# A decode step with two attention layers: the last head group's P.V split between rows and columns, and a new order around the softmax

## The chip, the cores and the metric

The kernel runs on one core of a Trainium2 chip. Its time is the device time of one execution in microseconds (us), and the median of three runs is quoted. A profile is one separate execution: its *span* runs from the first to the last instruction that the profiler recorded, and the execution's own time is a little longer. The engines are TensorE (PE, with its weight loads shown as PEld), VectorE (DVE), ScalarE (ACT), GpSimd (POOL) and SyncE (SP). SP issues every large load here, in one in-order queue (SPq in the profile). Sixteen DMA engines move the bytes.

## The reference

One token (batch 1, sequence 1, width 640) passes attention, an MLP block, the same attention again and the same block again. Weights and caches are the same both times.

```
W = 4096                                  # last W positions of the caches
q = (x @ wq).reshape(32 heads, 192)
k, v = k_cache[:, :, Sk-W:, :], v_cache[:, :, Sk-W:, :]
p = softmax(q . k * 192**-0.5)            # per head, over W
x = x + (p . v).reshape(6144) @ wo        # A, on layernorm(x)
x = x + B(layernorm(x))                   # B: x1 + gelu(layernorm(x1) @ w3) @ w4
x = x + A(...); x = x + B(...)            # second layer, same again
```

With a sequence of one position the shifts inside B move only padding zeros into place, so its first half adds nothing. Per head, K and V are 4096 x 192 bf16 each, 1536 KB. There are 32 heads and two layers.

## The kernel before

**Tiling.** The heads form eight groups of four (`G = 4`). A slot is an SBUF tile of 128 partitions x 6144 elements, which holds one head's K or V, 32 positions to a partition. There are fifteen slots; five hold `wq` for good. SP loads K and V into slots in a planned order (`plan`, L604): for each group the K of the next group and the V of this one alternate, with the 960 KB of `wo` in the middle, and the MLP weights `w34` (L125 to L138) last. `half` is a tile of half a slot; it holds the softmax's work areas (E, ET, O_lo, O_sb and one of two buffers of P) and, at the end of a layer, the last part of `w4`: L135 loads over E, L136 over the rest.

**One head's keys.** `trans` (L297) turns K on DVE in 32 x 32 blocks, in two halves of 128 x 1536 (L305). It writes into a spare slot, and K's slot is the spare of the next head. `kmm` (L326) multiplies with twelve matmuls (L331) into the scores S_ps, and its end frees the turned slot.

**The softmax of one group.** `soft_a`: maximum (L347), mask (L349), transpose on PE (L351), negated maximum (L353). `soft_b`: bias back to all partitions (L359, copied at L361), exponential into E with its sum (L363). `soft_c`: E is transposed on DVE (L369), sixteen small matmuls arrange P (L378), ACT copies it to SBUF as PT (L384), and the sum's reciprocal is taken (L386 to L390).

**P.V has two forms.** In rows (`pv_rows`, L426), 16 matmuls per head have eight columns of P as weights and stream V (L435, 128 x 384 each). The results of all heads of a group add up in one PSUM tile; `norm_rows` prepares the factors, and `evac_rows` (L465) evicts with ACT (L467, O_lo) and DVE (L468, O_sb), turns the result by f32 matmuls (L471 to L477) and casts it (L480). In columns (`pv_cols`, L396), V is the weights: 64 matmuls of one column each (L409, L415, L420), and a pair of heads is evicted by three short DVE instructions (`evac_cols`, L444). `outproj` (L483) multiplies a pair of heads with `wo`, 15 matmuls (L487).

**The order.** The schedule is written by hand: each engine takes its instructions in program order. While group g has its P.V in rows, the next group's keys are turned and multiplied, one head against one. Then come `soft_a` of the next group, both halves of the first K of the group after it, P.V of g's fourth head, `soft_b`, `evac_rows(g)`, both `outproj(g)`, and `soft_c`. The last group of a layer has all four heads in columns, with an eviction and an `outproj` after every second. The addition of L568 ends the attention; `mixer` (L570) does the MLP, with 60 matmuls on `w3` (L581) and 60 on `w4` (L598).

**Between the layers.** The second layer takes the groups backwards, so group 7 comes last and then first: its V and its turned K stay in eight slots. Two slots hold `w34`. No key can be loaded for the next layer until `mixer` has read `w3` and `w4` out of those two (L584, L601), and the next slots come free as `kmm` of group 7 ends, head by head. At this start (`warm`) the order is: `kmm` of four heads, `soft_a`, the query projection of the next group (L277 to L288), `soft_b`, both halves of the next group's first K, `soft_c`.

Of the kernel before, what the change touches and what calls it, by code (L numbers as in the profile page):

```python
# [8 lines left out]
BF16 = mybir.dt.bfloat16  # L9
F32 = mybir.dt.float32  # L10
U32 = mybir.dt.uint32
# [5 lines left out]
P = 128  # L17
G = 4
# [7 lines left out]
def kernel(  # L26
# [14 lines left out]
    nc = tc.nc  # L41
# [9 lines left out]
    J = W // P  # L51
    S4 = 4
    NJQ = J // S4
    NFB = Dh // 64
# [5 lines left out]
    HJ = J // 2  # L60
    HALF = FREE // 2
# [232 lines left out]
    T_t = {}  # L294
    spent = [None]

    def trans(h):  # L297
        Kn = resident.pop(("K", h))
        T = spent.pop()
        if T is None or T not in free:  # L300
            T = free.pop()
        else:
            free.remove(T)
        for hf in range(2):
            nc.vector.transpose(  # L305
                T[:, hf * HALF:(hf + 1) * HALF].bitcast(U32).rearrange(
                    "p (f j k) -> p j f k", f=NFB, j=HJ, k=32),
                Kn[:, hf * HALF:(hf + 1) * HALF].bitcast(U32).rearrange(
                    "p (j f k) -> p j f k", f=NFB, j=HJ, k=32))
        T_t[h] = T  # L310
        free.append(Kn)
        spent.append(Kn)
# [4 lines left out]
    def kmm(g, i):  # L317
        h = g * G + i
        if i == 0:
            S_t[g] = S_two[nS[0] % 2]  # L320
            nS[0] += 1
        S_ps = S_t[g]
        T = T_t[h]
        x, par = i // 2, i % 2
        n = 0
        for f in range(NFB):  # L326
            for t in range(2):
                for hf in range(2):
                    Tv = T[:, hf * HALF:(hf + 1) * HALF].rearrange("p (f c t) -> p f c t", f=NFB, t=2)
                    r = 32 * (2 * par + hf)  # L330
                    nc.tensor.matmul(  # L331
                        S_ps[r:r + 8, :], lhsT=Q_t[g][:, x, par * NCOL + 2 * f + t, :], rhs=Tv[:, f, :, t],
                        start=(x == 0 and n == 0), stop=(n == NCOL - 1), tile_position=(0, r),
                        skip_group_check=True)
                n += 1
        if h not in keep_T:
            free.append(T_t.pop(h))
# [26 lines left out]
            out=E, in_=S_ps[:], func=ACTF.Exp, bias=nb_sb[:, 0:1], scale=scale, accum_out=lpart[:, 0:1])  # L364
        sx[g].update(lpart=lpart)

    def soft_c(g):
        d = sx[g]
        nc.vector.transpose(  # L369
            ET.rearrange("p (j r) -> p j r", r=32), E.rearrange("p (j k) -> p j k", k=32))  # L370
        ETv = ET.rearrange("p (j u m) -> p j u m", u=8, m=4)
        Pv = Pp_ps[:].rearrange("p (x par hf j c) -> p x par hf j c", x=2, par=2, hf=2, c=8)
        for tl in range(4):
            par, hf = tl // 2, tl % 2
            for m in range(4):
                one = Pv[32 * m:32 * (m + 1), 0, par, hf, :, 2 * par:2 * par + 2]
                two = bass.AP(one.tensor, one.offset, [one.ap[0], [2 * G * J + 4, 2], *one.ap[1:]])
                nc.tensor.matmul(  # L378
                    two, lhsT=identb[:, 32 * tl:32 * (tl + 1)],
                    rhs=ETv[:, :, 0:2, m].rearrange("p (j e) x -> p x j e", e=2), start=True, stop=True,  # L380
                    tile_position=(0, 32 * m), skip_group_check=True)
        PT = PT_two[nP[0] % 2]
        nP[0] += 1
        nc.scalar.copy(PT, Pp_ps[:])  # L384
        lsel = sm.tile([P, G], F32, name="lsel")
        nc.vector.tensor_scalar(out=lsel[:], in0=hs[:], scalar1=d["lpart"][:, 0:1], scalar2=None, op0=ALU.mult)  # L386
        l_ps = psm.tile([P, G], F32, tag="psm", name="l_ps")
        nc.tensor.matmul(l_ps[:], lhsT=ones[:], rhs=lsel[:], start=True, stop=True)  # L388
        rl = sm.tile([P, G], F32, name="rl")
        nc.vector.reciprocal(rl[:], l_ps[:])  # L390
        d.update(rl=rl, PT=PT.rearrange("p (g j c) -> p g j c", g=G, c=8))

    O_t = {}
    nO = [0]

    def pv_cols(g, i, keep):  # L396
        h = g * G + i
        if i == 0:
            O_t[g] = O_two[nO[0] % 2]
            nO[0] += 1  # L400
        O_ps = O_t[g][:, 0:8].rearrange("p (a b) -> p a b", a=2)
        V = resident[("V", h)]
        PT = sx[g]["PT"]
        pr, odd = i // 2, i % 2
        oa = TB if odd else 0
        col = lambda j: PT[:, i, j // 2, 2 * i + j % 2:2 * i + j % 2 + 1]
        ca, cc = (3, 2) if odd else (0, 1)
        for j in range(J):
            nc.tensor.matmul(  # L409
                O_ps[:, pr, ca:ca + 1], lhsT=V[:, j * Dh + oa:j * Dh + oa + P], rhs=col(j),  # L410
                start=(j == 0), stop=(j == J - 1))
        r0 = TB if odd else 0
        oc = 0 if odd else P
        je = 0 if odd else J - 1
        nc.tensor.matmul(  # L415
            O_ps[r0:r0 + TB, pr, cc:cc + 1], lhsT=V[:, je * Dh + oc:je * Dh + oc + TB], rhs=col(je),
            start=True, stop=False, tile_position=(0, r0), skip_group_check=True)
        js = [j for j in range(J) if j != je]
        for j in js:
            nc.tensor.matmul(  # L420
                O_ps[:, pr, cc:cc + 1], lhsT=V[:, j * Dh + oc - r0:j * Dh + oc - r0 + P], rhs=col(j),
                start=False, stop=(j == js[-1]), skip_group_check=True)
        if not keep:
            free.append(resident.pop(("V", h)))

    def pv_rows(g, i, keep):  # L426
        h = g * G + i
        if i == 0:
            O_t[g] = O_two[nO[0] % 2]
            nO[0] += 1  # L430
        V = resident[("V", h)]
        PT = sx[g]["PT"]
        for jj in range(J // 2):
            r = 32 * (jj % 4)
            nc.tensor.matmul(  # L435
                O_t[g][r:r + 8, :], lhsT=PT[:, i, jj, :],
                rhs=V[:, jj * 2 * Dh:(jj + 1) * 2 * Dh], start=(i == 0 and jj < 4),
                stop=(i == G - 1 and jj >= J // 2 - 4), tile_position=(0, r), skip_group_check=True)
        if not keep:
            free.append(resident.pop(("V", h)))  # L440

    osb_t = {}

    def evac_cols(g, pr):  # L444
        if pr == 0:
            osb_t[g] = sm.tile([P, 2, 3], BF16, name="osb")
        osb, rl = osb_t[g], sx[g]["rl"]
        O_ps = O_t[g][:, 0:8].rearrange("p (a b) -> p a b", a=2)
        nc.vector.tensor_tensor(  # L449
            out=osb[:, pr, 0:3:2], in0=O_ps[:, pr, 0:4:3], in1=rl[:, 2 * pr:2 * pr + 2], op=ALU.mult)  # L450
        nc.vector.tensor_tensor(
            out=osb[0:TB, pr, 1:2], in0=O_ps[0:TB, pr, 1:2], in1=rl[0:TB, 2 * pr:2 * pr + 1], op=ALU.mult)
        nc.vector.tensor_tensor(
            out=osb[TB:P, pr, 1:2], in0=O_ps[TB:P, pr, 2:3], in1=rl[TB:P, 2 * pr + 1:2 * pr + 2], op=ALU.mult)
# [39 lines left out]
    def attention(order, xT_cur, xT_new, keep, loads):  # L494
# [13 lines left out]
        where = {what: n for n, what in enumerate(loads)}  # L508
        ahead = lambda *what: need(where.get(what, -1) + 1)

        def keys(h):
            if h not in T_t:
                ahead("K", h)
                trans(h)

        tot_ps, rstd = ln_stats(xT_cur)
        xn_bf = sm.tile([P, ND], BF16, name="xn_bf")
# [10 lines left out]
        if warm:  # L528
            need(G + 1)
        soft_a(g0)  # L530
        if warm:
            qproj(g1, xn_bf)
        soft_b(g0)
        if warm:
            keys(g1 * G)
        soft_c(g0)
        for n, g in enumerate(order):
            nxt = order[n + 1] if n + 1 < len(order) else None
            for i in range(G):
                if nxt is not None:  # L540
                    keys(nxt * G + i)
                    kmm(nxt, i)
                    if i == G - 1:
                        soft_a(nxt)
                        if n + 2 < len(order):
                            keys(order[n + 2] * G)
                ahead("V", g * G + i)
                if i == 1 and n + 2 < len(order):
                    qproj(order[n + 2], xn_bf)
                if nxt is not None:  # L550
                    if i == 0:
                        norm_rows(g)
                    pv_rows(g, i, ("V", g * G + i) in keep)
                    continue
                pv_cols(g, i, ("V", g * G + i) in keep)
                if i % 2 == 1:
                    evac_cols(g, i // 2)
                    ahead("wo", g)
                    outproj(g, i // 2, y_ps, n == 0 and i == 1, i == G - 1)
            ahead("wo", g)  # L560
            if nxt is not None:
                soft_b(nxt)
                evac_rows(g)
                outproj(g, 0, y_ps, n == 0, False)
                outproj(g, 1, y_ps, False, False)
                soft_c(nxt)
        need(len(loads))
        nc.vector.tensor_tensor(out=xT_new[:], in0=xT_cur[:], in1=y_ps[:], op=ALU.add)  # L568

# [99 lines left out]
```

## Time and profile before

| | us |
|---|---|
| median of 3 runs | 547.46 (547.16 to 548.74) |
| the profiled execution, own time | 548.08 |
| its span | 546.3 |
| PE busy / DVE busy / ACT busy | 321.1 / 272.9 / 35.3 |
| one half of a K transpose (L305), x120 | 1.751 each, 205.3 in all |
| bytes moved | 218.80 MB, mean 401 GB/s over the span |

Times inside the profile count from the span's start. "Idle before" a group is time in which its engine stood still just ahead of it, with what ended the wait. The granted TensorE clock is a share of full speed. A matmul's recorded duration holds pipeline time, so for a run of matmuls the distance from start to start tells more.

### The profile page before, as it was taken

What the parts mean: (1) busy time and instruction counts of PE and PEld (TensorE: products, weight loads), DVE (VectorE), ACT (ScalarE), POOL (GpSimd) and SP (SyncE); (2) the same over time, 40 slices, a digit from 0 to 9 for tenths busy, and PEclk for the clock granted to TensorE, in tenths of its full rate; (3) what the DMA queues carried; (4) which work ended last, traced back from release to release, by engine and by line L of the source; (5) the groups of instructions that cost most, each with busy time, mean ns of one, the idle gap of its engine ahead of it and who ended that gap; (6) DMA issues with size and microseconds to landing.
All of it is one profiled execution on the core that took longest, in us unless ns stands there. A gap on an engine that the chain in (4) does not pass through costs nothing.

```text
span 546.3 us, 8648 instructions
## 1 busy us (share of the span) xinstructions
PE 321.1 (59%) x3851; PEld 158.5 (29%) x3851; DVE 272.9 (50%) x394; ACT 35.3 (6%) x111; POOL 2.1 (0%) x11
## 2 busy tenths in 40 slices
PE   1164765675754667365575576766654667365575
PEld 0011232241322214131174233332322224131164
DVE  4176555555636545454312476775636545454312
ACT  1001010000100001010001001010100001010001
POOL 1000000000000000000000000000000000000000
PEclk9998757665577756557655677778677756557655
DMA  8999999999999999999996889999999999999992
GB/s 350 429 425 412 423 426 414 426 413 423 415 424 425 413 426 411 428 413 421 416 400 250 326 353 428 425 414 422 412 426 426 411 427 412 425 414 425 413 398 79
DMA packets 33833, 218.80 MB, mean 401 GB/s; under 512 B 2692, under 2 KB 16516, under 8 KB 17796
## 3 DMA queue, kind: packets, MB, share of 16 engines
q1 hardware_dynamic: 33786, 218.25, 97.0%
q8 instruction: 30, 0.49, 0.4%
q14 instruction: 7, 0.06, 0.0%
q10 hardware_dynamic: 10, 0.00, 0.0%
HBM read 218.24 MB, written 0.00 MB: 399 GB/s over the span
## 4 chain that ended last, share of the span: by engine, by line
DMA 53%; PE 21%; DVE 19%; issue 4%; SPq 1%; ACT 1%; DVEq 0%
DMA slot<-in_A_k_cache_dram 53%; DVE slot L305 14%; PE S_ps L331 9%; PE O_ps L435 2%; DVE pm L347 2%; PE O_ps L420 1%; PE O_ps L409 1%; SPq L108 1%; PE y_ps L487 1%; PE nb_ps L359 1%; PE qT_ps L277 1%; PE pmT_ps L351 1%; PE hT_ps L581 1%; PE y2T_ps L598 1%; DVE pmh L349 1%
## 5 line engine op out<-in xcount | busy, mean ns | idle before, releaser
L305 DVE STREAM_TRANSPOSE slot<-slot 128x1536 uint32<-128x1536 uint32 x120 | 205.3, 1751 | 78.9 <-DMA slot<-in_A_k_cache_dram 78.9
L331 PE MATMUL S_ps<-slot,Q 128*8 128x512 bf16 x768 | 170.4, 550 | 118.5 <-DVE slot L305 116.7
L331 PEld LDWEIGHTS <-Q 128*8 128x8 bf16 x768 | 42.8, 102 | 215.8 <-issue 203.3
L435 PE MATMUL O_ps<-slot,half 128*8 128x384 bf16 x512 | 61.4, 444 | 0.0
L435 PE MATMUL O_ps<-slot,PT 128*8 128x384 bf16 x384 | 42.0, 424 | 0.0
L347 DVE TENSOR_REDUCE pm<-S_ps 128x1 f32<-128x512 f32 x16 | 11.1, 691 | 42.4 <-PE S_ps L331 42.4
L361 ACT COPY nb_sb<-nb_ps 128x1 f32<-128x1 f32 x16 | 2.5, 159 | 399.4 <-PE nb_ps L359 399.4
L471 PE MATMUL OT_ps<-ho,half 128*128 128x2 f32 x28 | 8.0, 356 | 34.0 <-DVE half L468 34.0
L281 DVE TENSOR_TENSOR Xq<-qT_ps,maskq 128x24 bf16<-128x24 f32 x16 | 2.9, 182 | 48.6 <-PE qT_ps L277 48.6
L435 PEld LDWEIGHTS <-half 128*8 128x8 bf16 x512 | 19.4, 98 | 20.9 <-issue 17.6
L277 PE MATMUL qT_ps<-xn_bf,slot 128*128 128x1 bf16 x480 | 15.2, 164 | 14.0 <-DMA slot<-in_A_wq_dram 11.6
L277 PEld LDWEIGHTS <-slot 128*128 128x128 bf16 x480 | 13.8, 98 | 20.8 <-DMA slot<-in_A_wq_dram 13.3
L487 PE MATMUL y_ps<-osb,wo_g 128*128 128x1 bf16 x480 | 15.7, 165 | 4.7 <-DVE osb L480 3.7
L435 PEld LDWEIGHTS <-PT 128*8 128x8 bf16 x384 | 13.5, 97 | 15.4 <-issue 12.6
L487 PEld LDWEIGHTS <-wo_g 128*128 128x128 bf16 x480 | 15.9, 104 | 4.8 <-issue 4.5
L471 PEld LDWEIGHTS OT_ps<-ho,half 128*128 128x128 f32 x28 | 6.8, 303 | 35.2 <-DVE half L468 35.2
L351 PE MATMUL pmT_ps<-ident,pmh 128*4 128x128 f32 x16 | 5.2, 327 | 18.3 <-DVE pmh L349 18.3
L449 DVE TENSOR_TENSOR osb<-O_ps,rl 128x2 bf16<-128x2 f32 x4 | 0.6, 162 | 23.5 <-PE O_ps L420 23.5
L480 DVE CAST osb<-OT_ps 128x6 bf16<-128x6 f32 x14 | 2.3, 164 | 19.8 <-PE OT_ps L477 19.8
L390 DVE RECIPROCAL rl<-l_ps 128x4 f32<-128x4 f32 x16 | 2.9, 182 | 18.2 <-PE l_ps L388 18.2
L369 DVE STREAM_TRANSPOSE half<-half 128x512 bf16<-128x512 bf16 x16 | 11.2, 700 | 1.5 <-ACT half L363 1.5
L409 PE MATMUL O_ps<-PT,slot 128*128 128x1 bf16 x256 | 8.4, 165 | 5.5 <-issue 5.2
(116 smaller groups left out, 212.7 us busy)
## 6 DMA issues: line engine op xcount, KB each, us to landing
slot<-in_A_k_cache_dram SPq DMA_DIRECT2D x60, 1536.0 KB, 23.8
slot<-in_A_v_cache_dram SPq DMA_DIRECT2D x60, 1536.0 KB, 23.8
wo_g<-in_A_wo_dram SPq DMA_DIRECT2D x14, 960.0 KB, 28.5
slot<-in_A_wq_dram SPq DMA_DIRECT2D x5, 1536.0 KB, 13.0
slot<-in_B_w_dram SPq DMA_DIRECT2D x2, 1536.0 KB, 23.5
slot<-in_B_w_dram SPq DMA_DIRECT2D x2, 1120.0 KB, 19.5
half<-in_B_w_dram SPq DMA_DIRECT2D x2, 640.0 KB, 8.6
slot<-in_B_w_dram SPq DMA_DIRECT2D x2, 384.0 KB, 18.0
```

What stands on the lines that cost most here:

```text
L108: nc.sync.dma_start(t[:], (Kw if kind == "K" else Vw)(h))
L277: nc.tensor.matmul(qT_ps[:, tl:tl + 1], lhsT=wq_t[kc][:, t * P:(t + 1) * P], rhs=xn_bf[:, kc:kc + 1], start=(kc == 0), stop=(kc == ND - 1))
L305: nc.vector.transpose(T[:, hf * HALF:(hf + 1) * HALF].bitcast(U32).rearrange("p (f j k) -> p j f k", f=NFB, j=HJ, k=32), Kn[:, hf * HALF:( ...
L331: nc.tensor.matmul(S_ps[r:r + 8, :], lhsT=Q_t[g][:, x, par * NCOL + 2 * f + t, :], rhs=Tv[:, f, :, t], start=(x == 0 and n == 0), stop=(n ...
L347: nc.vector.tensor_reduce(out=pm[:], in_=S_t[g][:], op=ALU.max, axis=AX.X)
L349: nc.vector.tensor_scalar(out=pmh[:], in0=off[:], scalar1=pm[:, 0:1], scalar2=None, op0=ALU.add)
L351: nc.tensor.transpose(pmT_ps[0:G, :], pmh[:, 0:G], ident[:, :])
L369: nc.vector.transpose(ET.rearrange("p (j r) -> p j r", r=32), E.rearrange("p (j k) -> p j k", k=32))
L409: nc.tensor.matmul(O_ps[:, pr, ca:ca + 1], lhsT=V[:, j * Dh + oa:j * Dh + oa + P], rhs=col(j), start=(j == 0), stop=(j == J - 1))
L435: nc.tensor.matmul(O_t[g][r:r + 8, :], lhsT=PT[:, i, jj, :], rhs=V[:, jj * 2 * Dh:(jj + 1) * 2 * Dh], start=(i == 0 and jj < 4), stop=(i = ...
L471: nc.tensor.matmul(OT_ps[:, :, 0], lhsT=O_sb[:, 0:P], rhs=ho[:, 0:4:2], start=True, stop=True, skip_group_check=True)
L487: nc.tensor.matmul(y_ps[:, n:n + 1], lhsT=wo_t[g][:, 3 * pr + t, n * P:(n + 1) * P], rhs=osb[:, pr, t:t + 1], start=(first and t == 0 and ...
```

## The change

`trans` becomes `trans_begin` and `trans_end`, one half each, so that other DVE work can stand between the halves. `soft_c` takes the head whose second half it issues after the matmul of the sum. In the loop over groups the softmax of the next group is issued before the eviction and output product of this one: `soft_b` right after `soft_a`, ahead of the fourth P.V, and `soft_c` ahead of `evac_rows`. In the warm start, `soft_b` comes ahead of the query projection.

```
+            if i == G - 1:
+                soft_a(nxt)
+                soft_b(nxt)
+                if ahead_h is not None:
+                    keys(ahead_h, whole=False)      # first half only
             ...
+                pv_rows(g, i, kept(g, i))
             ahead("wo", g)
-            if nxt is not None:
-                soft_b(nxt)
-                evac_rows(g)
-                outproj(g, 0, ...); outproj(g, 1, ...)
-                soft_c(nxt)
+            soft_c(nxt, ahead_h)                    # second half inside
+            evac_rows(g)
+            if ahead_h is not None:
+                outproj(g, 0, ...); outproj(g, 1, ...)
```

The last group of a layer (`gz`; `g` is the one before it, whose output product is still to come) is taken out of the loop:

```
+        for i in range(2):
+            ahead("V", gz * G + i)
+            pv_rows(gz, i, kept(gz, i), n_heads=2)
+        outproj(g, 0, ...); outproj(g, 1, ...)
+        ahead("wo", gz)
+        norm_rows(gz)
+        ahead("V", gz * G + 2)
+        pv_cols(gz, 2, kept(gz, 2))
+        evac_rows(gz)
+        outproj(gz, 0, ...)
+        ahead("V", gz * G + 3)
+        pv_cols(gz, 3, kept(gz, 3))
+        evac_cols(gz, 1)
+        outproj(gz, 1, ...)
```

Rows and columns use the two O_ps buffers, one each. `evac_cols` gets an `osb` tile of its own. The warm start:

```
         soft_a(g0)
-        if warm:
-            qproj(g1, xn_bf)
         soft_b(g0)
         if warm:
-            keys(g1 * G)
-        soft_c(g0)
+            keys(g1 * G, whole=False)
+            qproj(g1, xn_bf)
+        soft_c(g0, g1 * G)
```

The loads and their slots stand in the same order on SP's queue. Only what two of them wait for differs: L136 overwrites O_lo and O_sb, whose last use is now the eviction of `gz` instead of `g`.

More of the change, by code (lines that the diff above doesn't have):

```diff
@@ L295, with trans_half, trans_begin @@
     spent = [None]
-    def trans(h):
+    half_t = {}
+    def trans_half(Kn, T, hf):
+        nc.vector.transpose(
+            T[:, hf * HALF:(hf + 1) * HALF].bitcast(U32).rearrange(
+                "p (f j k) -> p j f k", f=NFB, j=HJ, k=32),
+            Kn[:, hf * HALF:(hf + 1) * HALF].bitcast(U32).rearrange(
+                "p (j f k) -> p j f k", f=NFB, j=HJ, k=32))
+    def trans_begin(h):
         Kn = resident.pop(("K", h))
@@ L303, in trans, with trans_end @@
             free.remove(T)
[L304 to L309, printed above, removed]
+        trans_half(Kn, T, 0)
+        half_t[h] = (Kn, T)
+    def trans_end(h):
+        Kn, T = half_t.pop(h)
+        trans_half(Kn, T, 1)
         T_t[h] = T
@@ L365, in soft_b, with soft_c @@
         sx[g].update(lpart=lpart)
-    def soft_c(g):
+    def soft_c(g, h_next=None):
         d = sx[g]
@@ L388, in soft_c @@
         nc.tensor.matmul(l_ps[:], lhsT=ones[:], rhs=lsel[:], start=True, stop=True)
+        if h_next in half_t:
+            trans_end(h_next)
         rl = sm.tile([P, G], F32, name="rl")
@@ L394 @@
     nO = [0]
+    Oc_t = {}
     def pv_cols(g, i, keep):
         h = g * G + i
-        if i == 0:
-            O_t[g] = O_two[nO[0] % 2]
+        if g not in Oc_t:
+            Oc_t[g] = O_two[nO[0] % 2]
             nO[0] += 1
-        O_ps = O_t[g][:, 0:8].rearrange("p (a b) -> p a b", a=2)
+        O_ps = Oc_t[g][:, 0:8].rearrange("p (a b) -> p a b", a=2)
         V = resident[("V", h)]
@@ L424, in pv_cols, with pv_rows @@
             free.append(resident.pop(("V", h)))
-    def pv_rows(g, i, keep):
+    def pv_rows(g, i, keep, n_heads=G):
         h = g * G + i
@@ L437, in pv_rows @@
                 rhs=V[:, jj * 2 * Dh:(jj + 1) * 2 * Dh], start=(i == 0 and jj < 4),
-                stop=(i == G - 1 and jj >= J // 2 - 4), tile_position=(0, r), skip_group_check=True)
+                stop=(i == n_heads - 1 and jj >= J // 2 - 4), tile_position=(0, r), skip_group_check=True)
         if not keep:
@@ L444, in evac_cols @@
     def evac_cols(g, pr):
[L445 to L448, printed above, removed]
+        osb, rl = sm.tile([P, 2, 3], BF16, name="osb"), sx[g]["rl"]
+        osb_t[g] = osb
+        O_ps = Oc_t[g][:, 0:8].rearrange("p (a b) -> p a b", a=2)
         nc.vector.tensor_tensor(
@@ L509, in attention, with keys @@
         ahead = lambda *what: need(where.get(what, -1) + 1)
-        def keys(h):
-            if h not in T_t:
+        def keys(h, whole=True):
+            if h not in T_t and h not in half_t:
                 ahead("K", h)
-                trans(h)
+                trans_begin(h)
+            if whole and h in half_t:
+                trans_end(h)
         tot_ps, rstd = ln_stats(xT_cur)
@@ L530, in attention @@
         soft_a(g0)
-        if warm:
-            qproj(g1, xn_bf)
         soft_b(g0)
         if warm:
-            keys(g1 * G)
-        soft_c(g0)
-        for n, g in enumerate(order):
-            nxt = order[n + 1] if n + 1 < len(order) else None
-            for i in range(G):
-                if nxt is not None:
[L541 to L546, printed above, removed]
+            keys(g1 * G, whole=False)
@@ new lines, in attention @@
+            qproj(g1, xn_bf)
+        soft_c(g0, g1 * G)
+        kept = lambda g, i: ("V", g * G + i) in keep
+        for n, g in enumerate(order[:-1]):
+            nxt = order[n + 1]
+            ahead_h = order[n + 2] * G if n + 2 < len(order) else None
+            for i in range(G):
+                keys(nxt * G + i)
+                kmm(nxt, i)
+                if i == G - 1:
[3 more added lines that the diff above has]
+                        keys(ahead_h, whole=False)
@@ L547, in attention @@
                 ahead("V", g * G + i)
-                if i == 1 and n + 2 < len(order):
+                if i == 1 and ahead_h is not None:
                     qproj(order[n + 2], xn_bf)
[L550 to L559, printed above, removed]
+                if i == 0:
+                    norm_rows(g)
@@ L560, in attention @@
+                pv_rows(g, i, kept(g, i))
             ahead("wo", g)
-            if nxt is not None:
-                soft_b(nxt)
-                evac_rows(g)
+            soft_c(nxt, ahead_h)
+            evac_rows(g)
+            if ahead_h is not None:
                 outproj(g, 0, y_ps, n == 0, False)
                 outproj(g, 1, y_ps, False, False)
-                soft_c(nxt)
+        gz = order[-1]
+        for i in range(2):
+            ahead("V", gz * G + i)
+            pv_rows(gz, i, kept(gz, i), n_heads=2)
@@ L567, in attention @@
+        outproj(g, 0, y_ps, False, False)
+        outproj(g, 1, y_ps, False, False)
+        ahead("wo", gz)
[3 more added lines that the diff above has]
+        evac_rows(gz)
+        outproj(gz, 0, y_ps, False, False)
+        ahead("V", gz * G + 3)
+        pv_cols(gz, 3, kept(gz, 3))
+        evac_cols(gz, 1)
+        outproj(gz, 1, y_ps, False, True)
+        Oc_t.clear()
         need(len(loads))
```

## The prediction

> **What bounds the kernel now.** I read first the page's 40 slices, one slice 13.66 us.
>
> ```profile
> DMA  8999999999999999999996889999999999999992
> GB/s 350 429 425 412 423 426 414 426 413 423 415 424 425 413 426 411 428 413 421 416 400 250 326 353 428 425 414 422 412 426 426 411 427 412 425 414 425 413 398 79
> ```
>
> Inside a layer the DMA engines are full. They are not in slices 21 to 23 (between the layers) and in the last one. Next, stretches of 2 us there; the last two columns are DMA share and GB/s.
>
> ```profile
> 290.00:292.00 2.00, 0.59 (x2) 0.53 (x3) 0.63 (x4) 0.95 (x6) 0.00 (x0) 0.50 0.45 151
> 292.00:294.00 2.00, 1.74 (x60) 1.65 (x59) 0.44 (x3) 0.12 (x1) 0.00 (x0) 0.50 0.03 12
> 294.00:296.00 2.00, 0.41 (x16) 0.43 (x16) 0.91 (x5) 0.28 (x2) 0.00 (x0) 0.50 0.57 123
> 302.00:304.00 2.00, 2.00 (x20) 0.74 (x20) 0.00 (x0) 0.00 (x0) 0.00 (x0) 0.50 0.42 178
> 304.00:306.00 2.00, 2.00 (x28) 0.62 (x20) 0.00 (x0) 0.00 (x0) 0.00 (x0) 0.50 0.45 74
> 318.00:320.00 2.00, 1.67 (x15) 0.35 (x7) 1.30 (x1) 0.00 (x0) 0.00 (x0) 0.52 0.56 129
> ```
>
> Summing 1 minus the share over 288 to 320 us gives 8.6 us of idle DMA, in three holes: until L581 and L598 have read `w3` and `w4`, until `kmm` of group 7 frees slots, and until 317.8, when the first V can be issued. After 320 the share is 1.0 to the end of loads. So before 320 and after the last K, compute sets the time; in between, bytes do. The chain of waits from the last K:
>
> ```profile
> 513.40 0.70 DVE pm L347
> 514.88 1.38 PE O_ps L435 x16
> 516.26 0.53 PE nb_ps L359 x2
> 517.78 0.32 ACT half L467
> 518.12 0.43 DVE half L468
> 518.60 0.59 PE OT_ps L471 x2
> 520.19 0.94 PE y_ps L487 x30
> 521.13 0.38 PE Pp_ps L378 x14
> 521.53 0.59 ACT PT L384
> 524.92 1.53 issue
> 530.91 1.74 issue
> 535.33 0.17 DVE x L568
> ```
>
> The path from the scores to PT holds the previous group's fourth P.V, its eviction and its output product. Then four heads in columns pass, with two "issue" holes. The same stretch between the layers starts at 267.69 and ends at 289.45 (21.76 us against 21.93 here), with holes of 1.16 and 1.95.
>
> **The holes.** Counted in the built program's list of PE instructions, weight loads included, they stand at rows 3102 and 3358, and in the tail at 6776 and 7032: 256 rows apart, each time. The page's queue q8 shows 30 instruction packets for 0.49 MB, about 16 KB each, which is 256 times 64 bytes. So I read them as blocks of instructions that arrive late: from one crossing to the next is 6.2 us (280.93 to 287.13, 526.45 to 532.64) where PE could use up a block in 4.
>
> The Trainium skill, "Runtime: NRT & Kernel Launch" (Instruction fetch mechanics), has the same blocks of 256 but calls a crossing "mostly hidden". By it the holes would be something else, and would stay: 3.1 and 3.3 us less gain, some 546.5 in all. The rows decide here, since the distances fit.
>
> **The change, step by step, in the tail (times of before).**
> 1. L359 no longer waits for 16 matmuls of P.V: L353 ends at 514.92 + 0.28 = 515.20, L359 can start at 515.30 instead of 516.26: **-0.96**.
> 2. From the end of the exponential (517.78) to the cast L384 (521.53) are 3.75 us. After: transpose to first L378 0.72 (313.44 to 314.16 in the warm start), to the cast 0.47 (314.16 to 314.63), 0.06 of hand-over: 1.25. **-2.50**. PT is there at 522.12 - 3.46 = 518.66.
> 3. What was moved comes now: L467 0.41, L468 0.43 and hand-overs 0.11: 519.61. Then the turn, 518.60 to 519.95 without its cast, 1.3: 520.9. Two heads in rows, 2 x 1.38 (above): 523.67. L487 x30, 0.94: 524.6.
> 4. V of the third head. The landings are issue plus landing time: `wo` 493.56 + 27.5 = 521.1, the fourth V 506.1 + 22.4 = 528.5, so the third in the middle, 524.8. A wait of 0.3: 524.9.
> 5. Columns of head 3: 0.99 + 0.14 + 0.92, less 0.1 of overlap, 1.95: 526.85. The turn of the two row heads up to its first L487 is 1.59 (518.60 to 520.19): 528.45, its 15 matmuls 0.5: 528.95. The eviction's ACT and DVE part hides under L487 and the columns; uncovered it costs 0.95.
> 6. Columns of head 4, 2.05, three evictions to first L487 0.24, L487 0.65 and hand-over 0.02: 531.9, against 535.33: **-3.4**.
>
> The two holes are gone in this sum: 188 PE rows fewer per layer (two heads of 126 rows become 32). The next crossings fall 256 rows before the old ones, in the third head's columns (525.25) and at the last L487 (530.9). These are 5.7 us apart where 6.2 were needed: bounds 0 to 1.95 (the longest hole) a place, I take 0.1 to 0.5 in the tail and 0 between the layers, where the crossing falls into the first L487, 6.8 us after the one before.
>
> Changes between tile shapes (rows, columns, f32 turn): three more a place. The nearest row is L415, which takes 0.14 where its neighbours take 0.03: 0 to 0.33, inside the rounding of steps 3 and 5. By "TensorEngine Tiling (Array Packing)" (Key Properties) a change of tiling mode drains the array; it gives no time, and its sum would be this upper bound.
>
> **The edge of the stream.** `mixer` moves up by 3.4 too. L581 would start at 534.6; the last part of `w3` lands at 515.39 + 18.0 = 533.4. The last 24 of L598 would start at 542.43 - 3.4 = 539.0; L136 lands at 529.79 + 8.8 = 538.6:
>
> ```profile
> half<-in_B_w_dram SPq DMA_DIRECT2D x1, 640.0 KB, 8.8
> ```
>
> L136 now waits for the turn of the last group, about 528.2, before its issue at 529.79: 1.6 us to spare. So the tail can give at most 542.43 - 538.6 = 3.8.
>
> **Between the layers** the same sum gives 286.1 for 289.45: -3.35. The third V (251.18 + 27.8 = 279.0) and the fourth (262.2 + 20.6 = 282.8) come at the edge again, L136 at 284.47 + 8.4 = 292.9 against 293.2. Then the warm start. Before, the query projection, two halves (310.08, 3.43), and L369 follow one another; `kmm` of group 6 starts at 315.02. After: maximum known at 308.91, half one until 310.65, Xq, Qrep and Q until 311.5, L369 0.70, L386 0.19, half two 312.4 to 314.1; the exponential (310.45) and the projection run beside it. `kmm` starts at 314.15: **-0.87**. The first V's issue, which ends the third hole, moves with it. So 3.35 + 0.87 = 4.2 of the 8.6 us of idle DMA go, and the whole stream after it comes 4.2 earlier. Its lower bound is 0 (a hole refilled elsewhere). An upper one: `kmm` of group 7, 5.44 us at clock 0.50, took half at a clock near 1, 2.7 more.
>
> **Inside a layer** I cost the new order at nothing. The half that waits for K, and with it E's transpose, L378 and P.V, queues behind it on DVE as the whole did before; on PE, P.V of the fourth head waits about 0.9 behind L359, so one V slot is free 0.9 later. Cover: a load takes 23.8 us from issue to landing where its own transfer takes 3.7 (1536 KB at some 425 GB/s), 20 us of queue. If that were gone, 14 turns of 0.9 cost 12.6.
>
> **Sum.** 546.3 - 3.4 + 0.2 (the tail's crossing) - 4.2 = 538.9 of span. The profiled run's own time was 548.08, 0.6 above the median; taken from the median, 547.46 - 7.4 = **540.1**.
>
> **Rivals.**
> - *The stream's edge binds* (0.10): the V of heads 3 and 4 and L136 land later than worked out, or L136 loses its 1.6 us. For it: four landings within 0.5 us of use. Against: the same stream in the same order. With 2 us lost at each place: 544.1.
> - *The gain between the layers is refilled* (0.10): holes stay, as slots and not compute end them. For it: the third hole ends with a slot. Against: that slot waits for `kmm`, which moves. Tail alone: 547.46 - 3.2 = 544.3.
> - *The stream starves inside the layers* (0.04), the slower side: half one stands ahead of E's transpose on DVE and waits for K (longest wait 5.4), so PT, P.V and slot returns come late in 13 groups. It decides from 0.6 us a group (13 x 0.6 = 7.8 eats the gain); at 1.5 a group: 547.46 - 7.4 + 19.5 = 559.6. Against: the 20 us of queue.
>
> **How the numbers follow.** My forecast has 0.76, with 538.0 (faster clock, no waits) to 542.5 (one long hole at one place, edges 0.5 late). The rivals at 544 lie just above, so the range stops at 543. A run of this kernel can't tell less than 0.3% (1.6 us) from no change; both milder rivals are beyond that. Faster 0.94, within 0.3% 0.02, slower 0.04.
>
> **What would show it.** L568 to L347 (21.8) falls to about 18.5 in both places; no "issue" hole above 0.6 in P.V; idle DMA between the layers about 4.4; the last K lands near 503; share 1.0 inside the layers. Wrong if holes reappear at other rows, if L598 waits for L136, or if DVE's waits for K grow while the share falls below 1.

## The result and the profile after

The changed kernel takes 540.11 us (median of four runs, 538.62 to 540.43) against 547.31 us (545.67 to 548.74) for the kernel before: a ratio of 0.9864, 95% interval 0.9831 to 0.9897. On another chip the ratio was 0.9864 again (0.9845 to 0.9884). The forecast was 540.1 us, with a range of 538.0 to 543.0. The profiled execution has a span of 537.6 us against 546.3.

The page's 40 slices of the changed kernel (13.44 us each):

```profile
DMA  8999999999999999999999899999999999999995
GB/s 345 430 424 411 423 428 415 425 410 425 421 420 423 413 424 413 425 424 413 424 405 344 324 386 427 423 414 424 414 423 425 411 425 416 425 426 409 424 406 192
```

The digits no longer dip below 8 between the layers, and the last slice moves 192 GB/s where it moved 79. The second line of this fence is read against the same line of before: 250, 326 and 353 became 344, 324 and 386.

Stretches of 2 us of the changed kernel where the DMA engines are not full (the last three columns are granted clock, DMA share, GB/s):

```profile
290.00:292.00 2.00, 0.55 (x21) 0.47 (x18) 0.74 (x4) 0.39 (x2) 0.00 (x0) 0.50 0.67 194
298.00:300.00 2.00, 1.55 (x13) 0.50 (x16) 0.36 (x1) 0.00 (x0) 0.00 (x0) 0.50 0.80 334
300.00:302.00 2.00, 2.00 (x24) 0.72 (x20) 0.00 (x0) 0.00 (x0) 0.00 (x0) 0.50 0.00 0
302.00:304.00 2.00, 2.00 (x24) 0.56 (x12) 0.00 (x0) 0.00 (x0) 0.00 (x0) 0.57 0.83 233
314.00:316.00 2.00, 1.57 (x16) 0.50 (x11) 0.84 (x1) 0.00 (x0) 0.00 (x0) 1.00 0.74 174
```

The first hole, which waited for `mixer`, has almost gone. The second, where all slots wait for `kmm` of group 7, stays. The third shrank. Over 288 to 320 us they hold about 4.3 us of idle DMA instead of 8.6 (either figure shifts by some 0.3 with the width of the stretches that are summed).

The chain of waits in the tail of the changed kernel (new lines: L421 and L432 are the columns, L498 the output product, L591 the addition):

```profile
500.80 22.42 DMA slot<-in_A_v_cache_dram
523.22 0.04 issue
523.27 1.01 PE O_ps L421 x32
524.28 0.14 PE O_ps L427
524.42 0.93 PE O_ps L432 x31
525.35 0.02 issue
525.38 0.17 DVE osb L460
525.55 0.04 issue
525.59 0.22 PE y_ps L498 x3
525.81 0.05 issue
525.86 0.47 PE y_ps L498 x12
526.33 0.02 issue
526.36 0.17 DVE x L591
```

The chain no longer goes back through the softmax to the last K. It comes from a V: the fourth head's columns start when that V has landed. From the timeline of the same kernel:

```profile
519.53 0.96 PE L421 MATMUL O_ps<-PT,slot 128*128 128x1 bf16 x32 [0.63 <-DMA slot<-in_A_v_cache_dram]
...
523.27 1.01 PE L421 MATMUL O_ps<-PT,slot 128*128 128x1 bf16 x32 [0.33 <-DMA slot<-in_A_v_cache_dram]
```

The waits for V are 0.63 and 0.33 us, and the "issue" in front of the columns is down to 0.04 us. At the last output product, where a block of instructions ends, the chain has a pause of 0.05 us.

Where the 8.7 us of span between the two profiled executions come from. A place runs from the last maximum (L347, now L356) to the addition that ends the attention (L568, now L591).

| | before | after | difference |
|---|---|---|---|
| between the layers: maximum to addition | 21.76 | 18.09 | -3.67 |
| addition to the maximum of the warm start | 17.78 | 18.21 | +0.43 |
| that maximum to the issue of the first V | 10.55 | 9.30 | -1.25 |
| first V's issue to the turn of the last K | 189.56 | 188.48 | -1.08 |
| turn of the last K to the last maximum | 6.06 | 6.25 | +0.19 |
| tail: maximum to addition | 21.93 | 18.05 | -3.88 |
| addition to the end of `mixer` | 7.92 | 8.16 | +0.24 |

These, with +0.3 before the first row, add up to the difference of the spans. The fourth row is the stream inside a layer. It took 188.2 to 189.6 us in the twelve profiles of this study, with the kernel before at the upper end, and in two kernels that keep the old order in the loop it took 188.5 and 188.9 us, so most of its 1.08 is spread. This also brings the spans (8.7) and the medians (7.2) together.

### The profile page after: what moved, and what is told of

The parts are those of the page before. It is cut to its first block, busy times and chain, and to the rows that moved or that the text cites. A ratio compares the mean times of both kernels' runs of the same rounds, so it can differ in the third digit from the quotient of the medians.

```text
span 537.6 us, 8273 instructions
## 1 busy us (share of the span) xinstructions
PE 319.4 (59%) x3675; PEld 157.1 (29%) x3675; DVE 273.3 (51%) x398; ACT 36.3 (7%) x113; POOL 2.1 (0%) x11
## 4 chain that ended last, share of the span: by engine, by line
DMA 64%; DVE 18%; PE 15%; issue 2%; ACT 1%; SPq 1%; DVEq 0%
DMA slot<-in_A_k_cache_dram 50%; DMA slot<-in_A_v_cache_dram 14%; DVE slot L300 13%; PE S_ps L340 8%; DVE pm L356 1%; DVE half L378 1%; PE y2T_ps L621 1%; PE qT_ps L277 1%; PE hT_ps L604 1%; PE O_ps L447 1%; PE pmT_ps L360 1%; PE O_ps L421 1%; PE y_ps L498 1%; PE O_ps L432 1%; SPq L101 0%
## 5 line engine op out<-in xcount | busy, mean ns | idle before, releaser
L300 DVE STREAM_TRANSPOSE slot<-slot 128x1536 uint32<-128x1536 uint32 x120 | 206.8, 1756 | 89.9 <-DMA slot<-in_A_k_cache_dram 89.7
L340 PE MATMUL S_ps<-slot,Q 128*8 128x512 bf16 x768 | 173.2, 564 | 119.5 <-DVE slot L300 118.0
L340 PEld LDWEIGHTS <-Q 128*8 128x8 bf16 x768 | 45.0, 104 | 213.3 <-issue 203.4
L447 PE MATMUL O_ps<-slot,PT 128*8 128x384 bf16 x448 | 48.1, 435 | 0.0
L356 DVE TENSOR_REDUCE pm<-S_ps 128x1 f32<-128x512 f32 x16 | 11.1, 692 | 42.8 <-PE S_ps L340 42.8
L447 PEld LDWEIGHTS <-PT 128*8 128x8 bf16 x448 | 15.3, 99 | 16.6 <-issue 14.6
L482 PE MATMUL OT_ps<-ho,half 128*128 128x2 f32 x32 | 9.2, 356 | 17.0 <-DVE half L479 17.0
L498 PE MATMUL y_ps<-osb,wo_g 128*128 128x1 bf16 x480 | 15.6, 165 | 4.3 <-DVE osb L491 3.7
L498 PEld LDWEIGHTS <-wo_g 128*128 128x128 bf16 x480 | 15.6, 104 | 5.5 <-issue 3.9
L387 PE MATMUL Pp_ps<-half,identb 128*32 128x32 bf16 x256 | 6.7, 235 | 14.5 <-DVE half L378 14.5
L387 PEld LDWEIGHTS <-identb 128*32 128x32 bf16 x256 | 5.7, 115 | 20.5 <-issue 20.0
L372 ACT ACTIVATE half<-S_ps,nb_sb 128x512 bf16<-128x512 f32 x16 | 11.0, 687 | 0.5
```

Of the source, the lines that this page charges most:

```text
L300: nc.vector.transpose(T[:, hf * HALF:(hf + 1) * HALF].bitcast(U32).rearrange("p (f j k) -> p j f k", f=NFB, j=HJ, k=32), Kn[:, hf * HALF:( ...
L340: nc.tensor.matmul(S_ps[r:r + 8, :], lhsT=Q_t[g][:, x, par * NCOL + 2 * f + t, :], rhs=Tv[:, f, :, t], start=(x == 0 and n == 0), stop=(n ...
L356: nc.vector.tensor_reduce(out=pm[:], in_=S_t[g][:], op=ALU.max, axis=AX.X)
L372: nc.scalar.activation(out=E, in_=S_ps[:], func=ACTF.Exp, bias=nb_sb[:, 0:1], scale=scale, accum_out=lpart[:, 0:1])
L387: nc.tensor.matmul(two, lhsT=identb[:, 32 * tl:32 * (tl + 1)], rhs=ETv[:, :, 0:2, m].rearrange("p (j e) x -> p x j e", e=2), start=True, s ...
L447: nc.tensor.matmul(O_t[g][r:r + 8, :], lhsT=PT[:, i, jj, :], rhs=V[:, jj * 2 * Dh:(jj + 1) * 2 * Dh], start=(i == 0 and jj < 4), stop=(i = ...
```

## The experiments

Ratios are to the kernel before, run on the same chip; for the changed kernel it was 0.9864.

**The order without the rows.** The last group has its four heads in columns again, and the output product of the group before it goes back to its old place, ahead of them:

```
-        for i in range(2):
-            pv_rows(gz, i, kept(gz, i), n_heads=2)
-        ...
+        for i in range(G):
+            ahead("V", gz * G + i)
+            pv_cols(gz, i, kept(gz, i))
+            if i % 2 == 1:
+                evac_cols(gz, i // 2)
+                ahead("wo", gz)
+                outproj(gz, i // 2, y_ps, False, i == G - 1)
```

> The new order of the softmax and the split K transpose stay; the last group's four heads are in columns again, as before. Theory 'rows': the order only turns round what PE does one after the other (eviction and output product behind PT instead of ahead of it), so the columns start about 0.3 us earlier (PT at 518.66, then 0.95 + 1.3 + 0.94 on the path) and the late-instruction holes of 3.1 and 3.3 us stay; with 0.9 from the warm start, 1.5 us in all: about 545.8, idle DMA between the layers about 7.4. Rival 'order': PT 3.5 us earlier at both places is the gain: 541 to 542, with holes still there.

Measured: 546.12 us (545.66 to 547.03), ratio 0.9981 (0.9972 to 0.9990). Idle DMA between the layers was 8.5 us, where 7.4 was expected and the kernel before has 8.6. From the timeline:

```profile
281.72 0.68 PE L432 MATMUL O_ps<-PT,slot 128*128 128x1 bf16 x20 [1.79 <-issue]
287.92 0.22 PE L421 MATMUL O_ps<-PT,slot 128*128 128x1 bf16 x3 [1.93 <-issue]
```

The holes stay: 3.72 us here and 2.44 in the tail. The places take 22.05 and 20.79 us, where the kernel before has 21.76 and 21.93: between the layers a longer hole takes back more than the order gives. Without their holes they take 18.33 and 18.35, where the kernel before has 18.65 and 18.66. So the new order is worth 0.3 us a place, as theory "rows" has it. PT comes 3.5 us earlier, but the eviction and the output product that stood ahead of it now stand behind it on the same engine.

**The rows without the order.** The loop and the warm start of before, with the new last group:

```
-                    soft_b(nxt)
-                    if ahead_h is not None:
-                        keys(ahead_h, whole=False)
+                    if n + 2 < len(order):
+                        keys(order[n + 2] * G)
...
-            soft_c(nxt, ahead_h)
-            evac_rows(g)
+            soft_b(nxt)
+            evac_rows(g)
+            outproj(g, 0, ...); outproj(g, 1, ...)
+            soft_c(nxt)
```

> Only the last group's two heads in rows; softmax order, K transpose and warm start as before. Theory 'rows': PT as before at 8.8 us after L347, then 2.8 (rows) + 1.95 + 1.6 + 0.5 + 2.05 + 0.9 in place of 13.1: about 3.3 us less at each place, no hole: 540.7. Rival 'order': 1 us or less at each place, 545 to 546.

Measured: 541.26 us (540.58 to 542.26), ratio 0.9893 (0.9877 to 0.9909). The places take 18.32 and 19.24 us, the second with a wait of 0.25 for V and one hole of 0.46:

```profile
528.13 0.27 PE L432 MATMUL O_ps<-PT,slot 128*128 128x1 bf16 x5 [0.46 <-issue]
```

The rows alone bring most of the gain. And 18.32 is only 0.3 less than the 18.65 that the kernel before needs besides its holes: the two heads in rows hardly save work, they save the holes (in the tail 18.5 are left besides the hole and the wait, only 0.1 less than 18.66).

**The old warm start** in the changed kernel:

```
+        if warm:
+            qproj(g1, xn_bf)
         soft_b(g0)
         if warm:
-            keys(g1 * G, whole=False)
-            qproj(g1, xn_bf)
-        soft_c(g0, g1 * G)
+            keys(g1 * G)
+        soft_c(g0)
```

> The changed kernel with the old warm start (query projection ahead of soft_b, the next group's first K turned whole ahead of E's transpose). Theory: the first V after the layer change is issued 0.9 us later relative to the last kmm of group 7, and the time goes up by 0.9: 541.0, idle DMA between the layers up by 0.9 from 4.3. Rival: the warm start isn't on the path since the DMA refills another hole: within 0.3 us of the changed kernel, 540.1.

Measured: 541.01 us (540.39 to 541.89), ratio 0.9888 (0.9872 to 0.9904), idle DMA 1.3 us more. From the maximum to the issue of the first V it takes 10.56 us, as in the kernel before (10.55); the changed kernel takes 9.30. The difference of the medians is what theory says (0.9; by the ratios it is 1.3), but it can't be told from nothing by these intervals; the trace's 1.25 is the better witness.

**What the holes are.** The kernel before, with 128 more PE rows at the start, where PE waits for `wq`:

```
+    pad_ps = psm.tile([P, 1], F32, tag="psm", name="pad_ps")
+    for _ in range(64):
+        nc.tensor.matmul(pad_ps[:], lhsT=identb[:], rhs=identb[:, 0:1], start=True, stop=True)
```

> The kernel before with 64 extra matmuls (128 PE rows with their weight loads) at the very start, where PE waits for wq. They move every later PE row by 128 against blocks of 256. Theory 'blocks of instructions': the holes move 128 rows earlier in the work: none in the second and fourth heads' columns; one of about 1.6 us in the third head's L409 after some 25 matmuls between the layers; in the tail one of about 1.8 us in the third head's L409 after some 11, and perhaps one of up to 1.9 at the last L487. In all 3.1 becomes 1.6 and 3.3 becomes 1.8 to 3.7: 545.5 to 547.3. Rival 'holes belong to the data or to the column form': they stay in the second and fourth heads with 1.2 to 2.0 us each, and the time stays 547.3.

Measured: 545.24 us (543.39 to 545.90), ratio 0.9951 (0.9934 to 0.9967). The timeline between the layers (first line) and in the tail (L412 is the old L409, L490 the old L487):

```profile
283.32 0.33 PE L412 MATMUL O_ps<-PT,slot 128*128 128x1 bf16 x7 [0.93 <-issue]
526.07 0.70 PE L412 MATMUL O_ps<-PT,slot 128*128 128x1 bf16 x21 [0.94 <-issue]
532.54 0.25 PE L490 MATMUL y_ps<-osb,wo_g 128*128 128x1 bf16 x4 [2.01 <-issue]
```

There were 25 matmuls of the third head ahead of the first hole and 11 ahead of the second: the places named beforehand, to the matmul. The third hole came in the last output product, which was named too, behind 11 of its matmuls. The second and fourth heads have none. The holes belong to blocks of 256 PE rows, whatever the rows compute.

That the blocks arrive late shows in the same traces, in the times of the instruction packets on queue q8 (16 KB each). Each hole ends soon after such a packet has come in:

| kernel and place | packet on q8 (us) | hole ends | after the packet |
|---|---|---|---|
| before, between the layers | 278.41 to 279.50 | 280.93 | 1.43 |
| before, between the layers | 284.58 to 285.61 | 287.13 | 1.52 |
| before, tail | 523.99 to 525.09 | 526.45 | 1.36 |
| before, tail | 530.16 to 531.26 | 532.64 | 1.38 |
| 128 rows more, between the layers | 280.75 to 281.84 | 283.32 | 1.48 |
| 128 rows more, tail | 523.62 to 524.72 | 526.07 | 1.35 |
| 128 rows more, tail | 530.03 to 531.16 | 532.54 | 1.38 |

All 14 holes of 0.46 us or more that these two places show in the profiles of this study end 1.35 to 1.52 us after a packet. So PE waits there for its own instructions. Extra work made the kernel faster, by 0.5%: 3.11 us of holes between the layers became 0.93, and that place went from 21.76 to 19.45 us; in the tail 3.27 became 2.95. The holes at the third heads were 0.7 to 0.9 us smaller than expected. Each follows a crossing without a hole, which lies 5.2 and 5.3 us before the hole's end (counted back 256 rows along the timeline); after a crossing with a hole it was 6.2 and more.

**A delay between the layers**, in the changed kernel:

```
         outproj(gz, 1, y_ps, False, True)
+        if keep:                     # first layer only
+            for _ in range(4):       # 0.69 us each on VectorE
+                nc.vector.tensor_reduce(out=wait_sb[:], in_=S_two[0][:], op=ALU.max, axis=AX.X)
```

> The changed kernel with four extra VectorE reductions (0.69 us each, 2.8 us) right ahead of the addition that ends the first attention; the last output product hides some 0.55 of them, so compute between the layers is 2.2 us longer. Theory: compute there is paid one to one, through a later refill of the DMA: 542.3, idle DMA between the layers up by 2.2 from 4.3. Rival 'refilled': other holes shrink and less than 0.7 us is paid.

Measured: 542.31 us (542.00 to 543.31), ratio 0.9923 (0.9906 to 0.9939). The place took 20.51 us instead of 18.09, +2.42, and idle DMA between the layers went up by 2.6. The median is 2.2 us above that of the changed kernel; by the ratios, each on its own chip, the loss is 3.2 us, give or take 1.4 (both intervals taken together). Both are in line with one to one, and rival "refilled" (less than 0.7) falls. The first V's issue was 3.0 us later than in the changed kernel and the turn of the last K 3.7; 0.55 us of both was there before the place began.

**A delay inside the layers.** The same instruction on O_ps, four times in two groups of each layer, ahead of E's transpose:

```
             ahead("wo", g)
+            if n in (2, 4):
+                for _ in range(4):
+                    nc.vector.tensor_reduce(out=wait_sb[:], in_=O_two[nO[0] % 2][:], op=ALU.max, axis=AX.X)
             soft_c(nxt, ahead_h)
```

> The changed kernel with four extra VectorE reductions (about 0.55 us each) ahead of E's transpose in two groups of each layer: 8.8 us of VectorE time on the way to PT, all inside the layers. Theory: the queue of 20 us covers them, DMA share stays 1.0 and the time stays 540.1 within 0.5. Rival 'starved stream': up to 8.8 us are paid, 549.

Measured: 540.62 us (539.68 to 541.18), ratio 0.9887 (0.9870 to 0.9904); span 537.7. From the groups by line, and the wait of DVE for K:

```profile
L509 DVE TENSOR_REDUCE wait_sb<-O_ps 128x1 f32<-128x384 f32 x16 | 8.7, 545 | 0.4
...
DVE slot L300 <- DMA slot<-in_A_k_cache_dram: 81.8, 29, 7.1
```

There are 8.7 us more on DVE, ahead of PT, and the DMA share inside the layers stays at 1.0. DVE waits 81.8 us for K instead of 89.7: the delay came out of time in which it would have waited. That the span is the same to 0.1 is partly luck. Inside the layers this profile took 0.5 us more up to the first place and 0.7 more behind the first V's issue, and `kmm` of group 7 won 1.0 back (4.73 us for 5.75; the clock at 302 to 304 us was 1.00, in the changed kernel 0.57). By the ratios the loss is 1.3 us, give or take 1.4. So a loss of up to some 2.7 us isn't excluded; one of 8.8 is, and rival "starved stream" falls.

**The last wo behind the last V**, in the changed kernel; the first output product of the last group moves behind the fourth head's columns:

```
-                if i == 1:
+                if i == (G - 1 if g == order[-1] else 1):
                     loads.append(("wo", g))
...
         evac_rows(gz)
-        outproj(gz, 0, y_ps, False, False)
         ahead("V", gz * G + 3)
         pv_cols(gz, 3, kept(gz, 3))
+        ahead("wo", gz)
+        outproj(gz, 0, y_ps, False, False)
```

> The changed kernel with the last group's wo loaded behind its fourth V instead of behind the second, and the first output product of that group moved behind the fourth head's columns. The third and fourth V land 2.6 us earlier; bytes and their end are the same. Theory 'the stream's end binds the tail': the waits of L421 for V (0.63 and 0.33 in the tail) go, x is ready some 0.6 earlier, and L621 waits longer for the last part of w4 (L136), 0.7 instead of 0.15; the time falls by 0.3 at most: 539.8 to 540.1. Rival 'compute still binds': the whole 0.6 in the tail and 0.3 between the layers come through: 539.2.

Measured: 538.66 us (538.34 to 539.88), ratio 0.9857 (0.9836 to 0.9877). The time is below both expectations, but on that chip the kernel before was faster too (546.52); by the ratio it is 0.4 us below the changed kernel. Since the changed kernel hadn't run there, both ran once more, on one chip:

> The changed kernel itself, on the chip of the next run, so that the two can be compared: 0.9864 of the kernel before, between 0.983 and 0.990.

> The kernel with the late wo again. In its first profile the tail from the last maximum to the end of w4's product was 26.09 us against 26.21 in the changed kernel, and the stretch between the layers 25.77 against 26.12. Theory 'the stream's end binds': 0.3 to 0.5 us below the changed kernel, which is 0.1% and about what 5 rounds can't tell from nothing. Rival 'compute still binds': 1 us or more below it.

Measured: 539.65 (538.69 to 540.06) for the changed kernel and 539.26 (538.48 to 539.38) with the late wo; ratios 0.9864 (0.9845 to 0.9884) and 0.9855 (0.9837 to 0.9874). That is 0.4 us, the size expected. By these intervals it can be told neither from nothing nor from the 1 us of the rival; the traces tell more. The second kernel's timeline, between the layers (first line) and in the tail:

```profile
293.09 0.69 PE L621 MATMUL y2T_ps<-hT,half 128*128 128x1 bf16 x20 [0.60 <-DMA half<-in_B_w_dram]
524.54 0.46 PE L498 MATMUL y_ps<-osb,wo_g 128*128 128x1 bf16 x12 [1.10 <-issue]
532.98 0.50 PE L621 MATMUL y2T_ps<-hT,half 128*128 128x1 bf16 x13 [0.50 <-DMA half<-in_B_w_dram]
```

The waits for V are gone, and the sum of the attention is ready 1.0 us earlier between the layers (16.93 against 17.89 us after the maximum) and 0.7 in the tail. `mixer` then waits 0.60 and 0.50 us for the last part of `w4`. From the maximum to the end of `mixer` (its last addition) nothing is won: 25.85 us against 25.92 between the layers, 26.47 against 26.20 in the tail. So behind the changed kernel's compute stands the end of the stream, within half a microsecond, and "compute still binds" falls.

A block of instructions came late here, too: 1.10 us ahead of L498 in the tail, 1.40 in the first profile of this kernel. It vanished in the wait for `w4`, but it says something of the holes. It stands ahead of the last 12 matmuls, the row at which the changed kernel pauses for 0.05 us. The number of rows is the same; without the waits for V, and with the output products moved together, PE is at this row 1.6 us sooner after the maximum (15.88 us for 17.50) and the packet on q8 only 0.6 sooner (15.48 for 16.09). PE went on 1.50 us after the packet.

**The changed kernel with 128 more rows at the start** (the edit of the fourth experiment):

> The changed kernel with 64 extra matmuls (128 PE rows) at the very start, so that the crossings of blocks of 256 rows move by 128. Theory: between the layers they fall into the third head's columns (some 8 matmuls in) and the fourth head's (L432); the second is 5.4 us after the first where about 5.7 are needed: a hole of 0.3 to 0.6 there; in the tail into the rows of the second head and the first matmuls of the fourth head's columns, no hole above 0.3. Time 540.1 to 540.8. Rival: with fewer rows the position doesn't matter at all, no hole anywhere.

Measured: 539.82 us (538.63 to 540.94), ratio 0.9874 (0.9852 to 0.9896). One hole, of 0.17 us, in the fourth head's columns between the layers, at the line expected (the old L432); none in the tail:

```profile
284.87 0.43 PE L435 MATMUL O_ps<-PT,slot 128*128 128x1 bf16 x11 [0.17 <-issue]
```

It is smaller than theory had it (0.3 to 0.6) and far from what the kernel before shows; the rival, no hole anywhere, is nearly right here. But it isn't right in general that crossings cost nothing once there are fewer rows: the rows alone had 0.46 us in the tail and the late wo 1.10 and 1.40. What counts is the time between two crossings, and the changed kernel has just enough of it.

## Why the prediction was right

*The holes are late blocks of instructions and go:* shown. They moved by 128 rows when 128 rows were put ahead of them, each ends 1.35 to 1.52 us after a packet of instructions, and in the changed kernel the largest pause at a crossing is 0.05 us; I had charged 0.2 in the tail. That they go nearly to nothing is a close thing: the pause of 0.05 ends 1.46 us after its packet. My count was off a little: a head in columns shows 64 matmuls and as many weight loads in the trace, 128 rows and not 126. And the time from one crossing to the end of the next hole isn't fixed at 6.2 us; at the two holes above it was 5.2 and 5.3. "Runtime: NRT & Kernel Launch" (Instruction fetch mechanics) of the Trainium skill has the blocks of 256 right. Its "mostly hidden" does not hold in this stretch: 0.5 to 2.0 us a crossing in the kernels with four heads in columns.

*Steps 1 and 2 (L359 0.96 us earlier, 2.50 us off the way to PT):* in the tail L359 (now L368) starts 1.65 us after the maximum instead of 2.86, and the cast to PT 4.30 instead of 8.13: -1.21 and -2.62. The extra 0.4 us comes with the granted clock: 0.87 and 0.98 in 508 to 512 us, where the kernel before had 0.50 in its tail. Between the layers, at 0.50 in both, L368 and the cast start 1.75 and 4.62 us after the maximum, and the cast is 3.50 earlier than before, as in the sum (3.46).

*Steps 3 to 6 (what was moved is paid behind PT; addition 18.5 us after the maximum):* 18.05, and 18.18 in the second profile of the changed kernel. The rows started 6.96 us after the maximum where my sum has 7.5, and the third head's columns 11.22 where it has 11.5, after 0.63 us of wait for V. The sum holds to half a microsecond, but it hides what the first experiment shows: steps 1 and 2 give back nearly all that they bring. Read alone, "-0.96" and "-2.50" would have promised more than ten times the 0.3 us that the order is worth. The gain at each place is the holes (3.1 and 3.3), with 0.3 from the order and 0.1 to 0.3 from the rows' work.

*The edge of the stream:* near, as worked out. The third V came 0.3 us late between the layers and 0.63 in the tail, the fourth 0.33 late in the tail, and the product on `w4` (L598, now L621) lost 0.15 to L136 there. In the second profile of the changed kernel the waits for V add up to the same 1.2 us, and L621 lost nothing. I had worked out a most of 3.8 for the tail, and it gave 3.88 up to the addition and 3.6 up to the end of `mixer`.

*The warm start, -0.87:* mis-sized. It measured -1.25 at the first V's issue. My sum set the recorded durations on VectorE end to end; in the trace they overlap. E's transpose starts at 308.29 with 0.70, the next instruction at 308.92, and half two at 309.01, before that one's 0.19 are over. So half two is done 6.50 us after the maximum where my sum has 6.87:

```profile
308.29 0.70 DVE L378 STREAM_TRANSPOSE half<-half 128x512 bf16<-128x512 bf16 x1
308.92 0.19 DVE L395 TENSOR_SCALAR lsel<-hs,lpart 128x4 f32<-128x4 f32 x1
309.01 1.77 DVE L300 STREAM_TRANSPOSE slot<-slot 128x1536 uint32<-128x1536 uint32 x1
```

The first matmul of `kmm`, which needs only half one, had run by then too.

*Between the layers one to one, 4.2 of 8.6 us:* 4.3 of idle DMA went, and the first V was issued 4.2 us earlier. The delay of 2.4 us gave 2.6 more of idle DMA. `mixer` and `kmm` of group 7 took 0.43 us more than I allowed (`kmm` alone 5.75 us for 5.42), which nearly cancels the 0.4 that the warm start gave beyond my sum. That is luck: in other profiles the same matmuls of `kmm` took 4.55 to 5.74 us, by when the clock rose (4.55 with 1.00 at 302 to 304 us, where the changed kernel had 0.57).

*Inside a layer nothing:* shown to within some 2.7 us by the delay of 8.7 us. My sign of being wrong was that DVE's waits for K grow while the share falls below 1. They grew, from 78.9 to 89.7 us, but the share stayed at 1.0.

The rivals: "the stream's edge binds" was near but cost 1 us and not 4; "refilled" and "starved" were tested and fell.

*The number:* the mechanism and the size of its terms hold, but that 540.11 meets 540.1 is luck. Four runs of the changed kernel spread over 1.8 us, and the span of the profiled execution fell by 8.7 us where the sum has 7.4.

## What to carry to other kernels

Before an order is changed to make one result earlier, ask what else must still pass the same engine before the end: work that is only turned round is worth the overlap that it gains, here 0.3 of 3.5 us. Where a dense run of short instructions shows "issue" holes a fixed number of rows apart, count instructions, not work: fewer and larger ones, or even idle ones put elsewhere, move or shrink the holes, as long as enough time passes between two crossings. And in a kernel bound by a stream, look for the two or three places where the stream stands still; here compute was paid one to one there and, as far as the runs can tell, hardly anywhere else.

## What was not expected of the hardware

Sixty-four useless matmuls at the start made the kernel before 0.5% faster (0.9951, interval 0.9934 to 0.9967). From one crossing to the end of the hole at the next it took 6.2 us in the kernel before and in the one with the new order alone (281.72 to 287.92, 524.61 to 530.80), and up to 6.5 in the padded one (526.07 to 532.54), while the DMA engines were full (share 1.0). In these cases the next packet on q8 starts 3.6 to 4.0 us after PE has gone on, takes 1.0 to 1.1, and PE goes on 1.4 to 1.5 after its end. It looks as if only one block is fetched ahead; no run here tests that, nor why a packet starts when it does.
